# Gated attention, then routed experts: V as the stationary operand of the sums, squares moving 512 wide, and x turned back on its way through DRAM

## The chip, the cores and the metric

The kernel runs on one core of a Trainium2 chip. The metric is the device time of one execution in microseconds. Three runs of the kernel before took 2653.68 to 2654.44 us, with a median of 2654.0 us.

## The reference

Two stages follow each other. In the first, each of 8 batches has 2496 positions with rows u and v of 256 numbers and z of 64.

```python
scores = (1/S) * z @ z.T              # S = 2496, per batch
attn   = maximum(scores, 0) ** 2      # symmetric, as scores is
x      = u * (attn @ v)               # 8 x 2496 rows of 256
```

In the second, each of the 19968 rows of x goes to one of 8 experts, chosen by a hash of its token.

```python
e      = token_ids * 2654435761 % 8
out[i] = maximum(x[i] @ w1[e], 0) @ w2[e]   # w1: 256 x 1024, w2: 1024 x 256
```

Everything is fp32.

## The kernel before

**Tiles.** The positions of a batch are cut into tiles of P = 128: 19 whole tiles and one of R = 64 (tile TM = 19). Four tiles make a group, so a batch has NG = 5 groups of queries, the last of them with 3 whole tiles and the short one (448 queries). The loop runs over 40 groups (b, g). The word "step" below is one call of `between()`, the point at which the side work is given out; a group has 20 steps, and the variable `i` counts them.

**Scores** (L206 to L223). For a group, TensorE computes z z^T for key tiles that are not known yet: `fresh` (L184) lists the group's own tiles and all later ones. Each bank of 128 keys x 512 queries is cut at zero by ScalarE (L221, some by VectorE, L219) into a tile `a` in SBUF, and squared there in place by ScalarE (`square`, L226 to L241). In the last group the squares of the short query tile go into a tile of their own, `short`.

**The mirror.** The matrix is symmetric. Squares with keys of group a and queries of group g are also needed with the roles changed, so VectorE turns each tile of 512 x 512 in blocks of 32 x 32 into a tile `m` (L244 to L256, 16 transposes of 32 partitions x 512). Blocks within a group are turned in place (`own_turns`, L258 to L279). The turns wait in the list `to_turn`. `turn_scores` (L283) takes them off at each step by a budget in nanoseconds, 1450 a step while the sort runs and 1600 after it, at (elements + 170) each; `turn_now` (L294) does at once those that a sum is about to need.

**The sums** (`attend`, L333). For each key tile t and each query tile i, the square tile (128 keys x 128 queries) is the stationary operand, and V's 256 columns are the moving one:

```python
nc.tensor.matmul(acc[i // 2][:, i % 2, :], lhs(b, g, t, i), v_sb[b][:, t, :], ...)
```

The result has queries in the partitions. Two banks `acc` hold the four query tiles of a group. The first two key tiles (EARLY) and the last three (LATE) are done bank by bank, so that one bank can be emptied while the other is still in use. The short key tile is added by `attend_last` (L324), its two copies in the lower and upper 64 rows of the array. The short query tile is summed apart, in `attend_short` (L305), with 64 columns of the array for even and 64 for odd key tiles, and put together in `gate_short` (L314).

**The gate** (L341). VectorE multiplies a query tile of `acc` by u and by 1/S^2 into `x_sb`. GpSimd later scatters its rows with an indirect DMA to the row of `x_rows` in DRAM that the token's place in its expert gives (`place_x`, L557).

**The sort** (`places`, L380 to L541) computes these places in small operations, a few in each of the first 52 steps (SORT), on VectorE and GpSimd, with six small matmuls (L429).

**Loads.** SyncE issues them in the order of the program: z and V of the next batch at the groups 2 and 0, u of the next group at each group's start, the clearing of `x_rows` in the first 52 steps, and from the last group on the experts' weights (`load_w`, L621) and rows (`load_x`, L612).

**The experts** (from L703). Blocks of 512 rows, each followed by a block of 128 rows, each with one expert. `ups` (L725) computes h in banks of 512 columns with w1 as the stationary operand (L735), emptied by ScalarE (even) and VectorE (odd, L741); `down` (L744) multiplies by w2 (L747), ScalarE copies the result, and GpSimd scatters it to the output (L759). `turn_x` (L633) turns a block of x into the layout that `ups` needs. The first block may be read before the last group's rows are in place; in that case it is computed once more at the end.

Of the kernel before, what the change touches and what calls it, by code (L numbers as in the profile page):

```python
# [24 lines left out]
def kernel(  # L25
# [42 lines left out]
    c2 = (1.0 / S) ** 2  # L68
# [13 lines left out]
    xpool = pool("xpool", 3)  # L82

# [3 lines left out]


    slot_dram = nc.dram_tensor("slot_tokens", (P * NS,), I32)


    short = const.tile([P, T, R], F32)
    odd = const.tile([R, D], F32)
# [4 lines left out]
    nc.gpsimd.memset(short[R:P, TM, :], 0.0)  # L98
# [24 lines left out]
    zn, zT, v_sb, u_sb, x_sb, made, mirror, to_square, to_turn, gated = {}, {}, {}, {}, {}, {}, {}, [], [], []  # L123
# [24 lines left out]
    def load_v(b):  # L148
        v_sb[b] = vpool.tile([P, T, D], F32, name="v_sb")
        for g in range(NG):  # L150
            tiles_io(vf, b, group(g), v_sb[b][:, g * G:, :], False, nc.sync, twice=True)
# [21 lines left out]

    def whole(g):

        return range(G if g < NG - 1 else G - 1)
# [5 lines left out]


# [9 lines left out]
    def skipped(b, g, t):  # L193

        if t // G != g or b == 0 and not fine(g):
            return 0
        return (t % G if fine(g) else t % G // 2 * 2) * P

    def fine(g):


        return g > 1
# [3 lines left out]
    def scores(b, g):  # L206

        n = sum(width(t) for t in group(g))
# [17 lines left out]
    def square(n):  # L226
        for b, g, t in to_square[:n]:
            a = made[b, g, t // G][:, t % G, :]
            m = len(whole(g)) * P
            lo = skipped(b, g, t)  # L230
            pairs = [(a[:, lo:m], a[:, lo:m])] if lo < m else []
            if m < G * P:
                pairs.append((short[0:width(t), t, :], a[0:width(t), ds(m, R)]))
            for o, x in pairs:
                nc.scalar.square(o, x)  # L235
            if t % G == G - 1 and (t // G > g or b or fine(g)):
                turns = turns_of(b, g, t // G) if t // G > g else own_turns(b, g)
                to_turn.extend((n, (b, g, t // G), f) for n, f in turns)

                to_turn.sort(key=lambda e: min(e[1][2] - g, 2 if fine(g) else 1))  # L240
        del to_square[:n]  # L241


    def turns_of(b, a, g):  # L244

        def turn(r, c, m):
            if (b, a, g) not in mirror:
                mirror[b, a, g] = mirrors.pop(0)
            nc.vector.transpose(  # L249
                mirror[b, a, g][ts(c, Q)].rearrange("p t s q -> p (t s) q")[:, 0:m, ts(r, Q)],  # L250
                made[b, a, g][ts(r, Q)].rearrange("p t (s q) -> p (t s) q", q=P)[:, 0:m, ts(c, Q)])
        for r in range(NQ):
            for c in range(NQ):

                m = (len(group(g)) if r * Q < width(group(g)[-1]) else G - 1) * G
                yield m * Q, lambda r=r, c=c, m=m: turn(r, c, m)  # L256

    def own_turns(b, g):  # L258
# [7 lines left out]
        for r in range(NQ):  # L266
            for c in range(NQ):
                i, o = ts(r, Q), ts(c, Q)
                if g < NG - 1:
                    yield move(tiles[o, 2:4, 0:2, ts(r, Q)].rearrange("p s i q -> p i s q"), tiles[i, 0:2, 2:4, ts(c, Q)], 4)  # L270
                    if fine(g):
                        yield move(step[o, 0:3:2, ds(3 * P + r * Q, Q)], step[i, 0:3:2, ts(c, Q)], 2)
# [3 lines left out]
                if c * Q < R:  # L276

                    yield move(tiles[o, 3, 0:2, ts(r, Q)], short[i, ds(g * G, 2), ts(c, Q)], 2)
                    yield move(tiles[ds(R + c * Q, Q), 3, 2, ts(r, Q)], short[i, g * G + 2, ts(c, Q)], 1)  # L279
# [3 lines left out]
    def turn_scores(steps):  # L283
# [4 lines left out]
        while to_turn and turned > 0:  # L288
            n, _, f = to_turn.pop(0)
            f()  # L290
            turned -= n + 170
        turned = min(turned, 0)

    def turn_now(key):  # L294
        for e in [e for e in to_turn if e[1] == key]:
            to_turn.remove(e)
            e[2]()

    def lhs(b, g, t, i):

        if t in fresh(b, g):
            return made[b, g, t // G][:, t % G, ts(i, P)]
        return mirror[b, t // G, g][:, i, t % G, :]

    def attend_short(b):  # L305

        ps = mm_ps.tile([P, D], F32, name="q_ps", tag="mm")
        for t in range(T):
            a = short[:, t, :] if t in fresh(b, NG - 1) else lhs(b, NG - 1, t, G - 1)[:, 0:R]
            nc.tensor.matmul(ps[ds(t % 2 * R, R), :], a, v_sb[b][:, t, :],  # L310
                             start=(t < 2), stop=(t >= T - 2), skip_group_check=True)
        return ps

    def gate_short(b, ps):  # L314
        nc.scalar.copy(odd[:], ps[R:P, :])
        x = x_sb[b, NG - 1] = xpool.tile([P, G, D], F32, name="x_sb")
        nc.vector.tensor_add(odd[:], odd[:], ps[0:R, :])
        nc.vector.scalar_tensor_tensor(out=x[0:R, G - 1, :], in0=odd[:], scalar=c2, in1=u_sb[b, NG - 1][0:R, G - 1, :],
                                       op0=OP.mult, op1=OP.mult)
        gated.append((b * T + TM, x[0:R, G - 1, :]))  # L320

    def attend_last(b, g, acc):  # L324

        turn_now((b, TM // G, g))
        for i in (0, 2, 1, 3):
            if i in whole(g):
                h = ds(i // 2 * R, R)
                nc.tensor.matmul(acc[i // 2][:, i % 2, :], lhs(b, g, TM, i)[h], v_sb[b][h, TM, :],  # L330
                                 start=False, stop=False, skip_group_check=True)

    def attend(b, g, k, acc, queries):  # L333
        t = summed(b, g)[k]
        turn_now((b, t // G, g))
        for i in queries:
            if i in whole(g):
                nc.tensor.matmul(acc[i // 2][:, i % 2, :], lhs(b, g, t, i), v_sb[b][:, t, :],  # L338
                                 start=(k == 0 and i % 2 == 0), stop=(k == TM - 1), skip_group_check=True)

    def gate(b, g, i, acc):  # L341
        if i not in whole(g):
            return
        if (b, g) not in x_sb:
            x_sb[b, g] = xpool.tile([P, G, D], F32, name="x_sb")
        x = x_sb[b, g]
        nc.vector.scalar_tensor_tensor(  # L347
            out=x[:, i, :], in0=acc[i // 2][:, i % 2, :], scalar=c2, in1=u_sb[b, g][:, i, :],
            op0=OP.mult, op1=OP.mult,
        )  # L350
        gated.append((b * T + g * G + i, x[:, i, :]))
# [28 lines left out]
    def places():  # L380

        with tc.tile_pool(name="route", bufs=1) as route:
# [20 lines left out]
            room = sorting[:].rearrange("p t s q -> p (t s q)")  # L403
# [15 lines left out]
            yield  # L419
# [3 lines left out]
            yield  # L423
# [144 lines left out]
    nc.scalar.copy(odd[0:1, 0:1], zero[0:1, 0:1])  # L568
# [4 lines left out]
    load_v(0)  # L573
    load_tokens()
    load_u(0, 0)
# [7 lines left out]
    groups = [(b, g) for b in range(B) for g in range(NG)]  # L583
    place = places()
# [3 lines left out]
    def between():  # L588

        nonlocal i  # L590
        if i < SORT:
# [28 lines left out]
    def load_w(j, k):  # L620
        w1[j] = w_buf[2 * k][:].rearrange("p a b c -> p (a b c)").rearrange("p (h f) -> p h f", h=DP)  # L621
        w2[j] = w_buf[2 * k + 1][:].rearrange("p a b c -> p (a b c)").rearrange("p (c d) -> p c d", c=FP)
# [15 lines left out]
    mirrors = [mpool.tile([P, G, G, P], F32, name=f"m_{k}") for k in range(NG * NG // 4)]  # L638
# [3 lines left out]
    for n, (b, g) in enumerate(groups):  # L642
        if n + 1 < len(groups):
            load_u(*groups[n + 1])
        if g == 0 and b + 1 < B:
            load_v(b + 1)
        if g == 2 and b + 1 < B:
# [4 lines left out]
        acc = [acc_ps.tile([P, 2, D], F32, name="acc", tag="acc") for _ in range(2)]  # L652
# [185 lines left out]
```

## Time and profile before

| what | value |
|---|---|
| median of 3 runs | 2654.0 us |
| the profiled execution | 2655.1 us |
| its span, first to last instruction | 2653.2 us |
| granted TensorE clock, mean | 0.999 |
| first matmul of the sums | 17.9 us |
| first matmul of the experts | 1533.5 us |
| VectorE busy, 392 to 1488 us | 881 of 1096 us |
| ScalarE busy, same stretch | 324 of 1096 us |
| GpSimd busy, same stretch | 234 of 1096 us |

The profile is of one execution. A row of a group gives line, engine, operation, output and inputs by name, shape, count, then busy time and mean duration of one, and the idle time before. A row in order of time gives start, length and how many instructions it merges. TensorE shows two records for each fp32 matmul, and its weight loads stand as PEld. [...] A row of a stretch gives busy time and, in brackets, instructions of PE, PEld, DVE, ACT and POOL, then the granted clock, the share of the DMA engines' time and GB/s.

### The profile page before, as it was taken

What the parts mean: (1) busy time and instruction counts of PE and PEld (TensorE: products, weight loads), DVE (VectorE), ACT (ScalarE), POOL (GpSimd) and SP (SyncE); (2) the same over time, 40 slices, a digit from 0 to 9 for tenths busy, and PEclk for the clock granted to TensorE, in tenths of its full rate; (3) what the DMA queues carried; (4) which work ended last, traced back from release to release, by engine and by line L of the source; (5) the groups of instructions that cost most, each with busy time, mean ns of one, the idle gap of its engine ahead of it and who ended that gap; (6) DMA issues with size and microseconds to landing.
All of it is one profiled execution on the core that took longest, in us unless ns stands there. A gap on an engine that the chain in (4) does not pass through costs nothing. (4 is left out here: it accounts for less than half of the span.)

```text
span 2653.2 us, 32524 instructions
## 1 busy us (share of the span) xinstructions
PE 2643.0 (100%) x12054; PEld 2072.2 (78%) x12054; DVE 1394.5 (53%) x2907; ACT 598.1 (23%) x1304; POOL 495.9 (19%) x512
## 2 busy tenths in 40 slices
PE   9999999999999999999999999999999999999999
PEld 7788888888888888888878867777777777777777
DVE  7987888878878877887869811111111111111111
ACT  5115214222233133133142111111111111111111
POOL 1322122212221222222200111111111111111112
PEclk9999999999999999999999999999999999999999
DMA  4212112201220221112101276666666666666662
GB/s 167 63 32 71 39 30 70 51 21 67 51 71 17 51 71 39 37 63 52 33 18 31 63 184 165 162 156 161 154 155 157 155 152 165 164 165 163 166 156 84
DMA packets 288992, 256.74 MB, mean 97 GB/s; under 512 B 179100, under 2 KB 251821, under 8 KB 288832
## 3 DMA queue, kind: packets, MB, share of 16 engines
q1 hardware_dynamic: 268096, 213.55, 32.1%
q0 software_dynamic: 20736, 41.09, 4.6%
q8 instruction: 96, 1.57, 0.3%
q14 instruction: 64, 0.52, 0.1%
HBM read 208.91 MB, written 47.09 MB: 96 GB/s over the span
## 5 line engine op out<-in xcount | busy, mean ns | idle before, releaser
L249 DVE STREAM_TRANSPOSE m<-a 32x512 f32<-32x512 f32 (+1 forms) x1280 | 865.1, 676 | 21.0 <-ACT a L235 0.9
L338 PE MATMUL acc<-v_sb,a 128*128 128x256 f32 x3472 | 764.9, 380 | 0.0
L338 PEld LDWEIGHTS acc<-v_sb,a 128*128 128x128 f32 x3472 | 656.2, 190 | 96.9 <-issue 6.7
L741 DVE TENSOR_SCALAR hT<-h_ps 128x512 f32<-128x512 f32 x161 | 111.4, 692 | 946.2 <-PE h_ps L735 924.1
L735 PE MATMUL h_ps<-v_sb,m 128*128 128x128 f32 (+1 forms) x2080 | 567.7, 431 | 1.5 <-PEq L799 1.5
L747 PE MATMUL o_ps<-m,hT 128*128 128x256 f32 x2576 | 566.3, 379 | 0.0
L747 PEld LDWEIGHTS o_ps<-m,hT 128*128 128x128 f32 x2576 | 486.9, 190 | 77.6 <-issue 14.4
L338 PE MATMUL acc<-v_sb,m 128*128 128x256 f32 x2304 | 504.6, 380 | 2.8 <-DVE x_sb L347 2.8
L735 PEld LDWEIGHTS h_ps<-v_sb,m 128*128 128x128 f32 x2080 | 317.6, 191 | 235.6 <-issue 230.6
L338 PEld LDWEIGHTS acc<-v_sb,m 128*128 128x128 f32 x2304 | 438.7, 190 | 63.6 <-DVE x_sb L347 3.6
L221 ACT ACTIVATE a<-s_ps 128x512 f32<-128x512 f32 (+3 forms) x456 | 205.4, 592 | 851.1 <-PE s_ps L213 851.0
L557 POOL DMA_INDIRECT x_rows<-x_sb,slot_i x160 | 156.2, 976 | 1064.1 <-DVE x_sb L347 886.4
L759 POOL DMA_INDIRECT out_dram<-o_sb,idx x157 | 153.4, 977 | 918.1 <-ACT o_sb L754 910.1
L235 ACT ACTIVATE a<-a 128x512 f32<-128x512 f32 (+3 forms) x472 | 232.8, 651 | 0.0
L265 DVE STREAM_TRANSPOSE a<-a 32x128 f32<-32x128 f32 (+1 forms) x992 | 221.6, 248 | 8.8
L213 PE MATMUL s_ps<-zT 64*128 64x512 f32 (+1 forms) x960 | 195.0, 545 | 0.3 <-ACT zT L171 0.3
L754 ACT COPY o_sb<-o_ps 128x256 f32<-128x256 f32 x161 | 59.9, 372 | 595.4 <-PE o_ps L747 595.4
L739 ACT ACTIVATE hT<-h_ps 128x512 f32<-128x512 f32 x161 | 96.1, 597 | 368.8 <-PE h_ps L735 362.0
L213 PEld LDWEIGHTS s_ps<-zT 64*128 64x128 f32 x960 | 120.3, 186 | 71.2 <-issue 41.5
L545 POOL DMA_INDIRECT slot_tokens<-token,addr x160 | 156.1, 976 | 74.8 <-issue 48.5
L347 DVE SCALAR_TENSOR_TENSOR x_sb<-acc,u_sb 128x256 f32<-128x256 f32 x152 | 57.8, 420 | 194.3 <-PE acc L338 194.1
L635 DVE STREAM_TRANSPOSE v_sb<-v_sb 128x1024 f32<-128x1024 f32 (+1 forms) x65 | 53.9, 829 | 3.6 <-DMA v_sb<-x_rows 3.5
(101 smaller groups left out, 293.4 us busy)
## 6 DMA issues: line engine op xcount, KB each, us to landing
m<-in_moe_w_dram SPq DMA_DIRECT2D x260, 256.0 KB
m<-in_moe_w_dram SPq DMA_DIRECT2D x65, 1024.0 KB
v_sb<-in_v_dram SPq DMA_DIRECT2D x32, 512.0 KB
u_sb<-in_u_dram SPq DMA_DIRECT2D x32, 512.0 KB
v_sb<-x_rows SPq DMA_DIRECT2D x128, 128.0 KB
zn<-in_z_dram SPq DMA_DIRECT2D x28, 304.0 KB
v_sb<-x_rows SPq DMA_DIRECT2D x132, 32.0 KB
x_rows<-zero SPq DMA_DIRECT2D x8, 512.0 KB
```

What stands on the lines that cost most here:

```text
L213: nc.tensor.matmul(ps[:, lo:n], zT[b][h, ts(t, P)], zT[b][h, ds(g * G * P + lo, n - lo)], start=True, stop=True)
L221: nc.scalar.activation(a, ps[:, lo:n], AF.Relu)
L235: nc.scalar.square(o, x)
L249: nc.vector.transpose(mirror[b, a, g][ts(c, Q)].rearrange("p t s q -> p (t s) q")[:, 0:m, ts(r, Q)], made[b, a, g][ts(r, Q)].rearrange("p ...
L265: return n * Q, lambda: nc.vector.transpose(out, in_)
L338: nc.tensor.matmul(acc[i // 2][:, i % 2, :], lhs(b, g, t, i), v_sb[b][:, t, :], start=(k == 0 and i % 2 == 0), stop=(k == TM - 1), skip_gr ...
L545: st = nc.gpsimd.indirect_dma_start(out=slot_dram[:, None], out_offset=bass.IndirectOffsetOnAxis(ap=addr[0:n, c:c + 1], axis=0), in_=token ...
L557: st = nc.gpsimd.indirect_dma_start(out=x_dram[:, :], out_offset=bass.IndirectOffsetOnAxis(ap=slot_i[0:width(c % T), c:c + 1], axis=0), in ...
L735: nc.tensor.matmul(ps[:, ts(i, n)], w1[j][:, c, ts(k * m + i, P)], xT[j][:, :, c, :], start=(c == 0), stop=(c == DP - 1))
L741: nc.vector.tensor_scalar_max(o, ps[:], 0.0)
L747: nc.tensor.matmul(ps[:], hT[j][f][:, ts(t, P)], w2[j][:, f, :], start=(f == 0), stop=(f == FP - 1))
L759: st = nc.gpsimd.indirect_dma_start(out=out[:], out_offset=bass.IndirectOffsetOnAxis(ap=rows, axis=0), in_=o, in_offset=None, bounds_check ...
```

## The change

The roles in the sums change. V is now the stationary operand, and the squares move. V has 256 columns and the array 128, so the even columns go to one bank and the odd ones to the other, and all 512 queries of a group move at once. The result has V's columns in the partitions and queries along the bank: x comes out turned.

- `attend` and `attend_last` issue two matmuls for a key tile in place of four. In the last group of a batch a bank takes 448 queries in two matmuls of 256 and 192, and the short query tile is no longer summed apart: `attend_short`, `gate_short`, `short` and `odd` are gone.
- The queries in a bank are ordered by blocks of 32 rows (`p r i q`), and the mirror tiles have the layout `[P, NQ, G, G, Q]`, so that a turn writes 512 elements in one run. The turns are taken column first.
- The factor 1/S is put into the square.
- The gate turns each bank in blocks of 32 x 32 with VectorE into `x_q`, whose two halves are interleaved. Four DMAs write `x_q` to one of two DRAM buffers `x_way`, and three steps later four DMAs read it back as rows into `x_sb`, and GpSimd multiplies by u, one tile at a time. For the last group half of these DMAs are issued by ScalarE and VectorE multiplies.
- V of the next batch is loaded in five pieces in the groups 1 to 4 (V_LOADS), z in group 3, u at key tile 8 of its own group.
- The sort's pause before its counts is six steps in place of two.
- The weights of the second block of experts are loaded after the loop. The second block of experts starts when all of the first block's downs have been issued.
- `turn_scores` skips a turn for which no mirror tile is free. `CARRIED` is empty, so the path through `carry` is not used.

```diff
     def square(n):
         for b, g, t in to_square[:n]:
-            a = made[b, g, t // G][:, t % G, :]
-            ...
-            for o, x in pairs:
-                nc.scalar.square(o, x)
+            a = made[b, g, t // G][:, t % G, skipped(b, g, t):queries(g)]
+            nc.scalar.activation(a, a, AF.Square, scale=1.0 / S)
...
+    def squares(b, g, t):
+        if t in fresh(b, g):
+            a = made[b, g, t // G][:, t % G, :].rearrange("p (i r q) -> p r i q", r=NQ, q=Q)
+        else:
+            a = mirror[b, t // G, g][:, :, :, t % G, :]
+        parts, c = [], 0
+        for r in ([slice(0, NQ)] if TM not in group(g) else [slice(0, R // Q), slice(R // Q, NQ)]):
+            m = G if r.start < R // Q else G - 1
+            n = (r.stop - r.start) * m * Q
+            parts.append((slice(c, c + n), a[:, r, 0:m]))
+            c += n
+        return parts
...
-        for i in queries:
-            if i in whole(g):
-                nc.tensor.matmul(acc[i // 2][:, i % 2, :], lhs(b, g, t, i), v_sb[b][:, t, :],
-                                 start=(k == 0 and i % 2 == 0), stop=(k == TM - 1), skip_group_check=True)
+        for h in halves:
+            for cols, a in squares(b, g, t):
+                nc.tensor.matmul(acc[h][:, cols], v_sb[b][:, t, h::2], a,
+                                 start=(k == 0 and cols.start == 0), stop=(k == TM - 1), skip_group_check=True)
...
+    def gate(b, g, h, acc):
+        n = queries(g) // Q
+        if h == 0:
+            x_q[b, g] = qpool.tile([P, G * NQ, D // NQ], F32, name="x_q")
+        x = x_q[b, g]
+        nc.vector.transpose(x[:, 0:n, h::2], acc[h][:, 0:n * Q].rearrange("p (n q) -> p n q", q=Q))
+        if h == 0:
+            return
+        xs = xpool.tile([P, G, D], F32, name="x_sb")
+        o = x_way[g % len(x_way)]
+        ends = (b, g) == groups[-1]
+        queues = [nc.sync, nc.scalar if ends else nc.sync]
+        for a in range(NQ):
+            queues[a % 2].dma_start(o[:].rearrange("n p d -> p n d")[:, 0:n, ts(a, D // NQ)], x[ts(a, Q), 0:n])
+        def rows_of_x():
+            c = 0
+            for r in range(NQ):
+                m = G if r * Q < width(group(g)[-1]) else G - 1
+                queues[r % 2].dma_start(xs[ts(r, Q), 0:m], o[c:c + m].rearrange("i p d -> p i d"))
+                c += m
+            for k, t in enumerate(group(g)):
+                y = xs[0:width(t), k, :]
+                (nc.vector if ends else nc.gpsimd).tensor_mul(y, y, u_sb[b, g][0:width(t), k, :])
+                gated.append((b * T + t, y))
+        to_fetch.append((i + 3, None, rows_of_x))
...
-            yield
-            yield
+            for _ in range(6):
+                yield
...
+    V_LOADS = [(4, 4), (1, 9), (2, 9), (3, 6), (3, 12)]
...
             for t in range(TM - LATE, TM):
-                attend(b, g, t, acc, [2 * k, 2 * k + 1])
-            for q in (2 * k, 2 * k + 1):
-                gate(b, g, q, acc)
+                attend(b, g, t, acc, [k])
+            gate(b, g, k, acc)
...
+            if first < i == AHEAD:
+                while do:
+                    do.pop(0)()
...
+    load_w(work[1], 1)
     load_x(work[1], 1)
     run(work, 0, NM, NM + 2)
```

## The prediction

> **What bounds the kernel now.** I read the engine totals first, then who waits for whom, then the order of time on TensorE at a few places, then stretches. The totals, from part 1 of the page:
>
> ```profile
> PE 2643.0 (100%) x12054; PEld 2072.2 (78%) x12054; DVE 1394.5 (53%) x2907; ACT 598.1 (23%) x1304; POOL 495.9 (19%) x512
> ```
>
> TensorE is busy for 2643.0 of 2653.2 us. The list of waits holds only three entries with PE as the waiter worth a microsecond: 2.8 us for the gate's VectorE, 1.5 us at a branch, 1.2 us at the start. So a change can gain in two ways only: fewer or cheaper TensorE passes, or those few waits. Work on the other engines counts only where it newly makes TensorE wait. Each fp32 matmul appears as two records (two passes), so 19 key tiles x 4 query tiles are 152 records.
>
> What a pass costs is not its mean duration (380 ns is a latency; passes overlap) but the step from one start to the next. Rows of TensorE in order of time (start, length, count), from two stretches:
>
> ```profile
> 1550.76 13.98 PE L747 MATMUL o_ps<-m,hT 128*128 128x256 f32 x64
> ...
> 1533.46 8.75 PE L735 MATMUL h_ps<-v_sb,m 128*128 128x512 f32 x20
> ```
>
> 256 wide: (13.98 - 0.38 for the last one)/63 = 215.9 ns. 512 wide: (8.75 - 0.59)/19 = 429.5 ns. A pass of double width costs double: 431.8 against 429.5, 2.3 ns apart. Weight loads last 190 ns and hide under either. This decides the size of the case: moving squares 512 wide halves the instructions and loads of weights, but removes only those 2.3 ns for each pair of passes.
>
> **The sums, full groups.** 8 batches x 4 groups x 76 passes of 512 replace twice as many of 256: 2432 x 2.3 = 5.6 us less. The group rows would say otherwise:
>
> ```profile
> L338 PE MATMUL acc<-v_sb,a 128*128 128x256 f32 x3472 | 764.9, 380 | 0.0
> ...
> L735 PE MATMUL h_ps<-v_sb,m 128*128 128x512 f32 x1024 | 449.6, 592 | 1.5 <-PEq L799 1.5
> ```
>
> 449.6/1024 = 439.1 against 2 x 220.3 = 440.6, a gain of 3.6 us; with the mirror row (504.6/2304 = 219.0) it is a loss of 2.7 us. These rows count the tail of every run of passes in two groups at once, so I take the steps in time, and keep 0 as the other end.
> The moving squares are read in runs of 32 elements, as L735's xT already is at 429.5 ns, so I cost that at nothing.
>
> **The last group of a batch (448 queries).** Before: 114 passes x 215.9 = 24.6 us, and the 40 half-width passes of attend_short. In time, 24 of these took 2.69 us (1525.72 to 1528.41), so 40 take 4.5 us; together 29.1. After: 76 pairs of a 256- and a 192-wide pass. No row is 192 wide. The small block's 32 passes of 128 follow 32 of 512 in one run of 17.47 us: (17.47 - 0.28 - 32 x 0.4295)/31 = 111 ns. Halfway between 111 and 215.9 is 164 ns, and 76 x 379.9 = 28.9 us. Gain 0.2 us a batch, 1.8 us in all (0 to 3 by the roundness of these).
> The last key tile (L330) took 0.96 us a group (621.26 to 622.22). After, four passes of 512 run two at a time, as the scores do: 32 passes in 6.74 us (622.22 to 628.96), so 4 are 0.84, plus about 0.1 for entering the half-row form, which both have. I take 0, with -3.8 us as the other end.
>
> **Weights with a stride of 8 bytes.** V's even or odd columns are read every second element; no row of before has this. If it costs nothing, loads can follow each other every 111 ns (the 128-wide run shows it), below every pass. [...] If [...] the load took twice 111 = 222 ns, the full groups would still hide it (429.5), but the last group would not: max(215.9, 222) + max(164, 222) = 444 instead of 380, 64 ns x 608 pairs = 39 us. I take 0, because [...] the load has 190 ns of latency to spare under most passes.
>
> **VectorE.** Removed: 152 gates of 424 ns and 16 short ones (57.8 + 6.6 = 64 us). Added: 80 turns of a PSUM bank, 512 wide. Nearest rows: a transpose 128x512 takes 703 ns, an operation that reads 512 from PSUM 692 ns; 80 x 0.7 = 56 us. The turns of scores keep number and size (0.70 us); only their order and output layout move. VectorE is 80% busy in the steady stretch, so the total doesn't matter, but the moment does. The group boundary near 255 us:
>
> ```profile
> 255.02 3.19 PE L338 MATMUL acc<-v_sb,m 128*128 128x256 f32 x14
> 255.22 0.76 DVE L347 SCALAR_TENSOR_TENSOR x_sb<-acc,u_sb 128x256 f32<-128x256 f32 x2 [1.10 <-PE acc L338]
> ```
>
> The second bank is emptied by 255.98. TensorE starts the next group on the first bank at 255.02 and needs the second eight passes (1.73 us) later, at 256.75: slack 0.77 us. One turn of 0.70 to 0.76 us in place of two gates fits the same hole; a turn up to about 1.5 us would.
>
> ScalarE loses the short square and copy and gains nothing on the path; with 598 us busy I cost it at 0. GpSimd gains 160 multiplies. Its 1280-wide ones took 2.3 to 2.9 us, so 0.6 us each, 100 us hidden under 2150 us of idle time. They wait for DMAs, and sort operations and scatters queue behind them; nothing on TensorE needs those before the experts. SyncE gains 8 DMAs a group. The writes wait for VectorE's turn and the reads for the writes, and loads of u, v, z stand behind them; V is now loaded in five pieces 10 or more steps (17 us) ahead of its use, and u eleven steps. Cost 0.
>
> **The one stall, at 98 us.** Two stretches there:
>
> ```profile
> 98.00:104.00 6.00, 3.17 (x14) 2.15 (x13) 5.91 (x9) 2.84 (x7) 0.00 (x0) 1.00 0.00 0
> 104.00:110.00 6.00, 6.00 (x21) 4.94 (x21) 5.78 (x15) 0.00 (x0) 0.61 (x1) 0.72 0.67 145
> ```
>
> TensorE idled 2.83 us because VectorE was behind with turns and the sort, and the clock then fell to 0.72 for 6 us (1.7 us). Altogether 4.5 us. In the change the sort starts its counting four steps later. In VectorE's order the same 41 turns lie between the gates of the first two groups, with seven small operations more (7 x 0.2 = 1.4 us), while the 2.31 us reduction (L529) moves behind the second gate. First wait 0.5 + 1.4 = 1.9, second 2.5 - 2.3 + about 0.2 = 0.4: 2.3 instead of 2.8, the clock's share unknown. I take -1.0; ends -4.5 and +2.
>
> **Into the experts.** Now the last group's x goes out, comes back, is multiplied and only then scattered; the second block's weights are loaded after the loop. Before, the chain from the last gate (1533.66) to the second block's x in place was 7.7 us:
>
> ```profile
> 1541.32 0.45 DVE L635 STREAM_TRANSPOSE v_sb<-v_sb 128x256 f32<-128x256 f32 x1 [3.53 <-DMA v_sb<-x_rows]
> ```
>
> After: turn 0.7, write and read, each like that x load (issue 1538.07 to 1541.32, 3.3 us), four multiplies of 0.42, then the same 7.7: about 17 us. TensorE has 13.7 us of block 0's up and 13.8 us of its down first (27.5 us), and the downs are all put ahead of block 1. But VectorE waits inside this chain until about 9.5 us, with the emptying of h_ps behind it: with six banks of 1.72 us TensorE needs bank 1 back at 12.0 us. Slack 2.5 us. [...] The x rows go out in pieces of 256 bytes. The nearest row, the 256-byte loads above, is a read. By that row the slack stays 2.5 us[...]. 2 MB of weights at the 160 GB/s of that stage is 13 us, done by about 20. I take +0.5 (0 to +4).
>
> **Sum.** -5.6 - 1.8 - 1.0 + 0.5 = -7.9 us. The profiled execution took 2655.1 us (span 2653.2 and 1.9 around), so it becomes 2647.2; it lies 1.1 above the median, so the forecast is 2646 us.
>
> **Rivals.**
> A (forecast, 0.57): 2646, from 2642 to 2648.
> B (0.13): the stall at 98 us goes with its clock drop and the last key tile gains a little: -7.4 - 4.5 = about 2641. For it: the reduction has left the place between the gates. Against: more small work ahead of the first.
> C (0.14): the gain is real but spent elsewhere; entry to the experts +3, stall +1.5: about 2651. For it: chain slack of only 2.5 us. A change that does nothing measurable is this case too.
> D (0.11), other side: strided weights load at half rate. Place: the last group's 192-wide passes; price 39 us; 2646 + 39 = 2685. It turns the sign once the pair takes 393 ns, that is when loads step by about 177 ns, 1.6 times the 111. [...]
> E (0.05): the PSUM turn with its strided output takes 2 us, not 0.7: beyond 1.5 each boundary stalls, 0.5 x 39 = 20 us: 2666. Against: both nearest rows at 0.7.
>
> Faster by over 0.2% means below 2648.7: A and B, 0.70. C gives 0.14 within 0.2%, about what a measurement of this kernel can tell from no change. D and E give 0.16 slower. The range runs from 2637 (B with both unknown ends) to 2656 (C with its bounds) and leaves out D and E.
>
> **What would show it.** Right: 512-wide passes of the sums step by 429 to 430 ns, last-group pairs by about 380; no wait of TensorE for the turn beyond the one near 98 us; clock near 1.0. Wrong: pairs over 393 ns (D); a wait for the turn at every boundary (E); a gap of TensorE within 30 us of the experts' start (C); steps in the full groups that aren't 2 ns below two old ones, in which case the whole gain is missing.

## The result, and the profile after

The change made the kernel a little faster: 2645.2 us (median of 8 runs, 2643.37 to 2646.51) against 2653.9 (8 runs, 2653.44 to 2654.44). The ratio is 0.9967, with a 95% interval of 0.9956 to 0.9978. The profiled execution took 2645.0 us, its span is 2643.3 us, and the mean granted clock is 0.999, as before. The forecast was 2646 us.

The totals of the page after:

```profile
PE 2633.5 (100%) x9494; PEld 1627.3 (62%) x9494; DVE 1398.2 (53%) x2823; ACT 593.4 (22%) x1272; POOL 605.9 (23%) x667
```

TensorE executes 2560 records fewer, a fifth of the 12054, and is busy only 9.5 us less. VectorE is where it was, GpSimd gained 110 us. TensorE's rows of the sums, by form (count, then busy time and mean length of one):

```profile
L353 PE MATMUL acc<-a,v_sb 128*128 128x512 f32 x1664 | 728.7, 594 | 0.0
...
L353 PE MATMUL acc<-m,v_sb 128*128 128x256 f32 x512 | 152.3, 379 | 0.0
...
L353 PE MATMUL acc<-m,v_sb 128*128 128x192 f32 x512 | 125.1, 326 | 0.0
```

The lengths of one (594, 379, 326 ns) overlap and don't add up to the time; the steps do. TensorE in order of time (start, length, count), two runs of passes around the first group boundary and one in a last group:

```profile
101.41 15.59 PE L353 MATMUL acc<-m,v_sb 128*128 128x512 f32 x32 [2.89 <-DVE x_q L370]
116.84 13.90 PE L353 MATMUL acc<-a,v_sb 128*128 128x512 f32 x32
...
174.59 24.38 PE L353 MATMUL acc<-m,v_sb 128*128 128x256 f32 x128
```

The second row gives the new step: (13.90 - 0.59)/31 = 429.4 ns, against 431.8 for two old passes. The third row merges passes 256 and 192 wide in equal numbers: (24.38 - 0.38)/127 = 189 ns on average, or 378 for a pair. The first row is the one stall, and in the list of who waits for whom it is the only entry of more than 1.2 us with PE waiting:

```profile
PE acc L353 <- DVE x_q L370: 2.9, 1, 2.9
PE warm L611 <- POOL zero L96: 1.2, 1, 1.2
PE h_ps L775 <- ACTq L844: 0.9, 1, 0.9
```

By stage, read from the starts of the instructions (us). A batch runs from its first score matmul to that of the next one:

| stage | before | after | difference |
|---|---|---|---|
| start to the first score matmul | 8.76 | 8.68 | -0.08 |
| first batch, with the stall | 192.89 | 191.09 | -1.80 |
| six batches, each | 189.62 | 188.50 | -1.12 (-6.7 for six) |
| last batch, to the first expert matmul | 194.12 | 193.25 | -0.87 |
| experts | 1119.76 | 1119.27 | -0.49 |
| span | 2653.2 | 2643.3 | -9.9 |

Within a steady batch the four full groups give 4 x 0.18 = 0.73 us (the steps of a group's sums add up to 32.82 instead of 33.00), the sums of the last group 0.31, and the rest, with the last key tile, 0.09. The gain is there, small and evenly spread. The medians differ by 8.7 and the spans by 9.9, because the profiled execution before lay 1.2 us above its median.

The group boundary, VectorE in order of time (idle time and what ended it in brackets):

```profile
289.23 0.72 DVE L370 STREAM_TRANSPOSE x_q<-acc 128x512 f32<-128x512 f32 x1 [4.53 <-PE acc L353]
289.98 1.42 DVE L253 STREAM_TRANSPOSE m<-a 32x512 f32<-32x512 f32 x2
...
291.80 0.72 DVE L370 STREAM_TRANSPOSE x_q<-acc 128x512 f32<-128x512 f32 x1 [0.40 <-PE acc L353]
```

VectorE waits for TensorE before it turns each of the two banks, so here it isn't late; in all, it waits so before 71 of the 80 banks. Two turns of scores lie between the two banks, a detail that comes back below.

### The profile page after: what moved, and what is told of

It is laid out like the page before. It is cut to its first block, busy times and chain, and to the rows that moved or that the text cites. A ratio compares the mean times of both kernels' runs of the same rounds, so it can differ in the third digit from the quotient of the medians.

```text
span 2643.3 us, 27985 instructions
## 1 busy us (share of the span) xinstructions
PE 2633.5 (100%) x9494; PEld 1627.3 (62%) x9494; DVE 1398.2 (53%) x2823; ACT 593.4 (22%) x1272; POOL 605.9 (23%) x667
## 4 chain that ended last, share of the span: by engine, by line
PE 56%; issue 35%; POOL 6%; DVE 2%; POOLq 0%; DMA 0%; ACT 0%; ACTq 0%; SPq 0%; DVEq 0%
PE acc L353 47%; PE s_ps L219 7%; POOL out_dram L799 6%; PE acc L362 2%; DVE m L253 1%; POOLq L799 0%; PE warm L611 0%; DMA x_way<-x_q 0%; DMA x_sb<-x_way 0%; POOL x_rows L597 0%; DVE x_q L370 0%; DVE per_e L533 0%; DVE zn L525 0%; DVE per_e L537 0%; POOL v_sb L757 0%
## 5 line engine op out<-in xcount | busy, mean ns | idle before, releaser
L353 PE MATMUL acc<-a,v_sb 128*128 128x512 f32 (+2 forms) x1856 | 766.1, 570 | 0.0
L353 PEld LDWEIGHTS acc<-a,v_sb 128*128 128x128 f32 x1856 | 357.5, 196 | 378.8 <-issue 364.6
L353 PE MATMUL acc<-m,v_sb 128*128 128x512 f32 (+2 forms) x1792 | 530.2, 456 | 2.9 <-DVE x_q L370 2.9
L353 PEld LDWEIGHTS acc<-m,v_sb 128*128 128x128 f32 x1792 | 335.6, 197 | 196.7 <-issue 180.8
L389 POOL TENSOR_TENSOR x_sb<-x_sb,u_sb 128x256 f32<-128x256 f32 (+1 forms) x156 | 108.4, 724 | 928.1 <-DMA x_sb<-x_way 928.1
L280 DVE STREAM_TRANSPOSE a<-a 32x128 f32<-32x128 f32 (+2 forms) x1120 | 250.2, 248 | 10.2
L235 ACT ACTIVATE a<-a 128x512 f32<-128x512 f32 (+1 forms) x480 | 233.0, 646 | 0.0
L219 PEld LDWEIGHTS s_ps<-zT 64*128 64x128 f32 x960 | 110.2, 186 | 93.0 <-issue 62.9
L370 DVE STREAM_TRANSPOSE x_q<-acc 128x512 f32<-128x512 f32 (+1 forms) x80 | 56.3, 704 | 188.7 <-PE acc L353 188.4
```

The costliest lines, as they stand in the source:

```text
L219: nc.tensor.matmul(ps[:, lo:n], zT[b][h, ts(t, P)], zT[b][h, ds(g * G * P + lo, n - lo)], start=True, stop=True)
L235: nc.scalar.activation(a, a, AF.Square, scale=1.0 / S)
L280: return n * Q, lambda: nc.vector.transpose(out, in_)
L353: nc.tensor.matmul(acc[h][:, cols], v_sb[b][:, t, h::2], a, start=(k == 0 and cols.start == 0), stop=(k == TM - 1), skip_group_check=True)
```

## The experiments

Each experiment changes the kernel after; its ratio compares its median with that of the kernel before on the same chip. Chips differ a little: the kernel before took 2654.2 to 2655.6 us on those used here.

**Squares 256 wide again.** The change with its 512 columns moved in two parts:

```diff
-        for r in ([slice(0, NQ)] if TM not in group(g) else [slice(0, R // Q), slice(R // Q, NQ)]):
-            m = G if r.start < R // Q else G - 1
+        for r in [slice(0, R // Q), slice(R // Q, NQ)]:
+            m = G if r.start < R // Q or TM not in group(g) else G - 1
```

> The changed kernel, its squares moving 256 wide: V still stands, every key tile of a full group takes two matmuls for each half of V. Theory (a pass costs its columns and a fixed 2.5 ns, so width gives the full groups their gain): 2432 passes of 429.2 ns become 4864 of 215.9, so 2.5 ns each, +6.1 us; the last group is unchanged. Span 2649 us, clearly nearer to the kernel before. Rival (the gain comes from V standing still, from the boundaries or from the other engines, and width is nothing): no difference, span 2643 us.

Measured: 2651.2 us, ratio 0.9988 (0.9981 to 0.9994), 6.0 above the change (5.7 when each is set against the kernel before on its own chip); a steady batch takes 189.28 us, 0.78 more. In order of time:

```profile
307.64 13.98 PE L353 MATMUL acc<-a,v_sb 128*128 128x256 f32 x64
```

64 passes fill 13.98 us where 32 wide ones fill 13.90: (13.98 - 0.38)/63 = 215.9 ns. So the width of the moving operand is worth the 2.3 ns a pair, and this makes up most of the result.

**Columns of V without a stride.** Each bank takes 128 columns side by side in place of every second one, in both sums; the columns of x are then in another order.

```diff
-                nc.tensor.matmul(acc[h][:, cols], v_sb[b][:, t, h::2], a,
+                nc.tensor.matmul(acc[h][:, cols], v_sb[b][:, t, ts(h, P)], a,
```

> The changed kernel, but the halves of V are columns 0 to 127 and 128 to 255, read without a stride; the columns of x come out in another order. Theory (a stride of 8 bytes is free): time within 1 us of the changed kernel, 192-wide passes at 160 to 164 ns as now; weight loads may fall from 196 to 190 ns, which is hidden. Rival (the stride costs something, in the 192-wide passes of the last group): 608 pairs get faster by some ns each, a gain of 1 to 3 us.

**Every fourth column.** The weights have a stride of 16 bytes and reach into the next key tile, so the sums are of other numbers (the last key tile stays as it is).

```diff
-                nc.tensor.matmul(acc[h][:, cols], v_sb[b][:, t, h::2], a,
+                nc.tensor.matmul(acc[h][:, cols], v_sb[b][:].rearrange("p t d -> p (t d)")[:, t * D + h:t * D + h + 4 * P - 3:4], a,
```

> The changed kernel, but each weight load of the sums takes every fourth element of V (16 bytes apart, over two key tiles), so the sums are of other numbers; attend_last keeps its stride of 8 bytes. Theory A ([...] at least double): loads step by 222 ns or more, full groups hide it, last-group pairs go from 378 to at least 444 ns, +40 us or more, span 2683 us or above. Theory B ([...] the stride is nothing): span 2643 us, last-group pairs at 378 ns.

Measured: 2644.2 us without a stride (0.9962, 0.9948 to 0.9976), and 2703.7 us with 16 bytes (1.0186, 1.0170 to 1.0201). The rows of weight loads, of the change, of no stride, and of 16 bytes (last but one number: mean ns of one):

```profile
L353 PEld LDWEIGHTS acc<-a,v_sb 128*128 128x128 f32 x1856 | 357.5, 196 | 378.8 <-issue 364.6
```

```profile
L353 PEld LDWEIGHTS acc<-a,v_sb 128*128 128x128 f32 x1856 | 346.6, 190 | 389.1 <-issue 372.6 <-ACT a L235 7.4 <-ACT a L227 3.8
```

```profile
L353 PEld LDWEIGHTS acc<-a,v_sb 128*128 128x128 f32 x1856 | 555.1, 311 | 199.3 <-issue 6.4
```

Eight bytes cost 6 ns a load and next to no time: a batch takes 188.50 against 188.42 us, 0.7 us for all eight. Sixteen cost 121 ns a load. Where it hurts is seen in a last group with 16 bytes, TensorE in order of time:

```profile
179.66 26.01 PE L353 MATMUL acc<-m,v_sb 128*128 128x256 f32 x111
```

(26.01 - 0.37)/110 = 233 ns a pass where the change has 189: here the load, not the pass, sets the step. The theory's doubling, to 222 ns or more, was my own estimate, twice the 111 ns at which 128-wide passes stepped before, and comes near. In the full groups it is hidden: passes still step by (19.91 - 0.59)/45 = 429 ns, read at 619.68 us. A batch is 7.2 us longer, 58 for eight. So the slower load that the prediction feared shows at 16 bytes, where it sets a step of 233 ns, and not at 8, where the last group steps by 189. Why 16 bytes are slow and 8 are not, no run shows.

**No way through DRAM.** The eight DMAs of a group are left out, and GpSimd multiplies what the gate wrote by u as it lies, so the products aren't rows of x.

```diff
-        for a in range(NQ):
-            queues[a % 2].dma_start(o[:].rearrange("n p d -> p n d")[:, 0:n, ts(a, D // NQ)], x[ts(a, Q), 0:n])
...
-                queues[r % 2].dma_start(xs[ts(r, Q), 0:m], o[c:c + m].rearrange("i p d -> p i d"))
...
-                (nc.vector if ends else nc.gpsimd).tensor_mul(y, y, u_sb[b, g][0:width(t), k, :])
+                k0 = k if t < TM else 0
+                z = x[0:width(t), k0 * NQ:k0 * NQ + NQ].rearrange("p n d -> p (n d)")
+                (nc.vector if ends else nc.gpsimd).tensor_mul(y, z, u_sb[b, g][0:width(t), k, :])
```

> The changed kernel without the way through DRAM: GpSimd multiplies the turned tile x_q itself by u, so the rows that are scattered are not the rows of x. All eight DMAs a group are gone. Theory (the detour is wholly hidden): span within 1 us of 2643.3; at the experts' start VectorE is free about 9 us earlier, with nothing gained. Rival (the detour's DMAs slow weights, squares or the experts' entry): a gain of 2 us or more.

Measured: 2645.2 us, ratio 0.9967 (0.9954 to 0.9979), the change's own time, with batches of 188.50 us. The detour is wholly hidden.

**The detour's DMAs twice.** Each write and each read is issued a second time.

```diff
-        for a in range(NQ):
+        for a in [*range(NQ)] * 2:
...
-                queues[r % 2].dma_start(xs[ts(r, Q), 0:m], o[c:c + m].rearrange("i p d -> p i d"))
+                for _ in range(2):
+                    queues[r % 2].dma_start(xs[ts(r, Q), 0:m], o[c:c + m].rearrange("i p d -> p i d"))
```

> The changed kernel, each of the detour's DMAs issued twice. Theory: nothing in the groups; at the experts' start the chain of write and read gets about 3 us longer, VectorE comes back to h_ps at about 14 us in place of 10.9 after the first expert matmul, TensorE needs bank 1 at 12.0 us and waits 2 to 3 us once; span about 2646 us. Rival (DMA traffic itself is in the way of TensorE or of loads): losses spread over the groups, 5 us or more, and waits of TensorE for DMAs. Second rival (slack larger than reckoned): 0.

Measured: 2664.0 us, ratio 1.0036 (1.0023 to 1.0050). The six batches between still take 188.50 us; the loss is the last batch, 202.74 instead of 193.25, the experts, 1128.7 instead of 1119.3, and 1.6 us in the first batch. But the main place isn't the one expected. TensorE's longest wait and, below it, SyncE's issues in order of time:

```profile
PE h_ps L776 <- DVE v_sb L679: 9.3, 1, 9.3
```

```profile
1504.10 11.00 SPq L386 DMA_DIRECT2D x_sb<-x_way  x8
...
1528.69 1.92 SPq L660 DMA_DIRECT2D v_sb<-x_rows  x4
```

TensorE waits 9.3 us at its first expert matmul, for block 0's x (v_sb), not at bank 1. The eight reads hold SyncE for 11.00 us, because each second read waits until the first has landed in the same tile (SyncE's list of waits has `x_sb<-x_way` 8 times there, 15.8 us in all). Their rows are scattered later, and the load of block 0, which waits for that scatter in both kernels (8.5 us here, 9.3 without the doubling), is issued at 1528.7 us instead of 1515.6. That chain had been on no list of mine. In the experts TensorE then waits 1.8 us for a bank and 2.5 us for weights, and its first 24 passes take 13.1 us. So a bank is waited for, as expected, but one of ScalarE's, and for less time than block 0's x.

**The same, but not in the last two groups.**

```diff
-        for a in [*range(NQ)] * 2:
+        for a in [*range(NQ)] * (2 if groups.index((b, g)) < len(groups) - 2 else 1):
...
-                for _ in range(2):
+                for _ in range(2 if groups.index((b, g)) < len(groups) - 2 else 1):
```

> The detour's DMAs doubled in all groups but the last two. Theory (the loss of the doubled run came at the experts' entry alone, by the last two groups: x of the group before last is scattered later, so block 0's x comes too late): span within 2 us of 2643.3, no wait of TensorE at the first expert matmul. Rival (the doubled traffic costs in the groups): about 2655 us or more.

Measured: 2681.6 us, ratio 1.0092 (1.0077 to 1.0108), on a chip on which the kernel before took 2655.6. The end behaves as the theory said: the last batch takes 193.26 us, and no wait stands before the first expert matmul. But the steady batches took 191.1 to 196.6 us, 34 us more in all, with waits of the sums for squares and for the turns of banks:

```profile
PE acc L353 <- ACT a L235: 12.2, 6, 2.8
PE acc L353 <- DVE x_q L370: 6.9, 8, 4.2
```

The run before had the same doubling in the same groups and 188.50 us in each batch, so the doubled traffic as such, the rival here, isn't shown to be the cause. What differs in the traces is ScalarE: while it cuts scores at zero between 220 and 1500 us it stands still 37 times, for 0.2 to 1.5 us, 24.6 us in all, where the run before has not one such stop. Near 405 us, for one, its scores were ready, and SyncE's issues and VectorE's turns of z stood as in the run before, which speaks against late loads. What it waited for the profile doesn't name. From this pair only the place of the first one's loss is taken.

**Each bank turned twice, and three times.** The edit for twice; three times has `range(3)`.

```diff
-        nc.vector.transpose(x[:, 0:n, h::2], acc[h][:, 0:n * Q].rearrange("p (n q) -> p n q", q=Q))
+        for _ in range(2):
+            nc.vector.transpose(x[:, 0:n, h::2], acc[h][:, 0:n * Q].rearrange("p (n q) -> p n q", q=Q))
```

> The changed kernel, each bank turned twice into the same tile, so that emptying a bank takes 1.43 us of VectorE in place of 0.72. Theory (the second bank has 0.8 us of slack at each group boundary): no stall at the boundaries, only the one near 98 us longer by about 1 us; span 2643 to 2645 us. Rival (VectorE is already at its limit at 80%, and any work added to it shows): 80 x 0.72 = 57 us more work, a loss of 10 us or more.

> The changed kernel, each bank turned three times, 2.15 us. Theory: the second bank is then late by 2.15 - 0.72 - 0.8 = 0.65 us at each of 39 boundaries, some 25 us in all, span about 2669 us, and the list of waits names TensorE waiting for the turn at every boundary. Rival (the slack is larger[...]): under 5 us.

Measured: twice 2664.2 us (1.0038, 1.0024 to 1.0051), three times 2720.0 us (1.0247, 1.0231 to 1.0263). Both are dearer than the theory's slack allowed. TensorE's waits, first with each bank turned twice, then three times (us in total, times, longest):

```profile
PE acc L353 <- DVE x_q L371: 11.5, 25, 4.3
```

```profile
PE acc L353 <- DVE x_q L371: 60.9, 40, 4.7
```

And one boundary with each bank turned twice, VectorE and TensorE in order of time:

```profile
293.06 1.47 DVE L371 STREAM_TRANSPOSE x_q<-acc 128x512 f32<-128x512 f32 x2 [3.97 <-PE acc L353]
294.56 1.42 DVE L253 STREAM_TRANSPOSE m<-a 32x512 f32<-32x512 f32 x2
...
296.01 1.47 DVE L371 STREAM_TRANSPOSE x_q<-acc 128x512 f32<-128x512 f32 x2
...
297.63 1.53 PE L353 MATMUL acc<-m,v_sb 128*128 128x512 f32 x3 [0.32 <-DVE x_q L371]
```

From the start of the first bank's turn to TensorE's need of the second bank are 297.63 - 0.32 - 293.06 = 4.25 us (six passes for the late key tiles and four for the early ones, about 10 x 0.43). In it must fit two gates, the two turns of scores between them, and small gaps: 2T + 1.42 + 0.21. That gives a limit of T = 1.31 us, not 1.5, because the first bank's turn and the scores delay the second's. At T = 1.47 the sum is over by the 0.32 us of this wait, from which it was read. The test is three times (2.15 to 2.2): over by some 1.7 us a boundary by this sum, and a steady batch grew by 9.15 us, 1.8 for each of its five boundaries.

**Twice, with the turns of scores moved behind the second bank.** Beside the doubling:

```diff
-            turn_scores(1 if k else 0.8)
+            if k:
+                turn_scores(1.8)
```

> Each bank turned twice as before (1.43 us), but the turns of scores that stood between the two banks' turns are handed out after the second. Theory (in the doubled run the second bank was late because first bank's turn 1.43 + two score turns 1.43 = 2.86 us did not fit in the 2.58 us in which TensorE does the last three key tiles of the second half; without them the second turn starts on time and ends 1.63 us after the next group's first pass, 0.1 us before it is needed): the waits at the boundaries vanish, only the first stall near 98 us is longer than in the changed kernel, by 1 to 2 us; span 2644 to 2647 us. Rival (VectorE's total load decides): still about 2660 us.

Measured: 2663.0 us, ratio 1.0030 (1.0019 to 1.0041). The waits at the boundaries are nearly gone, 4 in place of 25:

```profile
PE acc L353 <- DVE x_q L371: 6.8, 4, 4.8
```

Yet the time is only 1 us better (2 us by the ratios), and over 14 us above the theory. The first batch took 196.0 us where doubling alone took 194.2. Five of the six steady batches took 189.7 to 190.0 us, where doubling alone took 190.6 and the change 188.5, and one took 191.2, on the chip that also made the batches of the early doubling uneven. So the two turns between the banks seem to account for 0.8 of the 2.1 us that doubling costs a steady batch. At three boundaries of one of these batches the second bank is still late: its first two passes step by 0.53 and 0.51 us in place of 0.43. That moving the turns pays isn't shown.

**The stall: turns held back, and given back.** In the group with the stall, VectorE's budget for turns is cut at three steps; in the second kernel it is given back over six later ones.

```diff
-        turned += steps * (1600 if i >= SORT else 1450)
+        turned += steps * (0 if 33 <= i < 36 else 1600 if i >= SORT else 1450)
```

```diff
-        turned += steps * (1600 if i >= SORT else 1450)
+        turned += steps * ({33: 700, 34: 0, 35: 0}.get(i, 1600 if i >= SORT else 1450)) + (682 if i in (44, 47, 50, 60, 64, 68) else 0)
```

> The changed kernel with no turns handed out in the three steps before the end of the second group (steps 33 to 35), about six turns of 0.71 us moved behind that gate. Theory (the stall near 98 us is VectorE's queue of turns and sort work ahead of the gate; 4.4 us late at the first bank): the wait and the clock's dip go, -4 to -4.7 us, span about 2639 us, unless the turns held back make the next boundary late (then up to 2 us of it are lost). Rival (the stall is the sort's own chain, or would be paid later in full): span 2643 us or more.

> The changed kernel with about five turns held back in the three steps before the end of the second group, and six handed out again one by one in the third and fourth group (steps 44 to 68), where VectorE was seen idle for 2.9 and 2.8 us. Theory (the stall near 98 us is only the order of VectorE's work, and the earlier attempt lost its gain because the six turns stayed behind to the end of the batch): no stall near 98 us and none near 194 us; span about 2638.6 us, 4.5 us below the changed kernel. Rival (VectorE has no room in the first batch, and the debt comes up wherever it is put): a wait of 2 to 4 us at another boundary, span 2642 us or more.

Measured: 2646.5 us (0.9969, 0.9956 to 0.9981) and 2647.0 us (0.9964, 0.9951 to 0.9978). TensorE's wait after each, in the first and in the second:

```profile
PE acc L362 <- DVE a L280: 3.6, 1, 3.6
```

```profile
PE acc L353 <- DVE x_q L370: 2.0, 1, 2.0
```

The stall near 98 us is gone in both. In the first, a wait of 3.6 us stands at 194 us in its place, with VectorE busy for 5.76 of the 6 us from 192 us on: the turns held back were never given back, and the batch's last turns came late. In the second, a wait of 2.0 us stands at 172 us. It looks like the same debt, and its time is the rival's, but the stretch shows another thing (busy time of PE, PEld, DVE, ACT, POOL):

```profile
170.00:174.00 4.00, 2.40 (x11) 1.56 (x9) 1.61 (x4) 0.00 (x0) 1.50 (x2) 1.00 0.01 0
```

VectorE is busy for 1.61 of 4 us. It stood idle for 2.34 us before the turn that TensorE waited for, and the profile doesn't name what it waited for, as with ScalarE's stops in the early doubling, on the same chip. So the first kernel speaks for turns put off and not given back being paid later; that VectorE has no room in the first batch isn't shown by either.

**Where VectorE's time went.** VectorE, then GpSimd, of the kernel after in order of time, some 14 us before the stall:

```profile
83.92 1.60 DVE L533 TENSOR_TENSOR per_e<-m,per_e 128x8 f32<-128x8 f32 x1
85.56 0.17 DVE L534 TENSOR_TENSOR per_e<-per_e 128x8 f32<-128x8 f32 x1
...
86.99 1.52 DVE L537 TENSOR_TENSOR per_e<-per_e 128x8 f32<-128x8 f32 x1
```

```profile
83.18 2.32 POOL L536 TENSOR_TENSOR zn<-zn,per_e 128x1280 f32<-128x1280 f32 x1
85.58 2.90 POOL L540 TENSOR_TENSOR zn<-zn 128x1280 f32<-128x1280 f32 x1
```

Operations of one size, 128x8, take 0.17 us or nine times that. The long ones end with GpSimd's: 83.92 + 1.60 = 85.52 against 83.18 + 2.32 = 85.50, and 88.51 against 88.48. Two transposes on VectorE, with one input each, take 1.30 us meanwhile, as two took at 86.22 us in the kernel before, where GpSimd ran nothing. The kernel before has the same: its L493 took 1.93 us and its L497 1.31 us, beside the same two GpSimd operations. That the long ones waited for GpSimd's to end is read from the ends that fall together; why they would, no trace shows. So 1.43 + 1.35 = 2.8 us of VectorE's time are lost just ahead of a stall of 2.9.

**The sort's small operations out of the way.** One comparison goes ahead of GpSimd's long operations; the three others on the same tile go to GpSimd itself; the small operations that follow from their result go to the end of the sort.

```diff
+            nc.vector.tensor_tensor(late, upto[:, :, C - G - 1], thr, op=OP.is_ge)
             nc.vector.tensor_tensor(total, rank, wide(thr), op=OP.is_ge)
...
-            nc.vector.tensor_tensor(late, ahead, thr, op=OP.is_ge)
-            nc.vector.tensor_mul(late, late, jump)
+            nc.gpsimd.tensor_mul(late, late, jump)
...
-            nc.vector.tensor_add(late, late, start)
-            nc.vector.tensor_add(late, late, ahead)
+            nc.gpsimd.tensor_add(late, late, start)
+            nc.gpsimd.tensor_add(late, late, ahead)
```

> The changed kernel with the sort's small operations of two inputs taken out of GpSimd's way: the comparison (L533) stands ahead of GpSimd's long operations, the product and two sums that follow are done by GpSimd itself, and the minimum, the flags and the count come at the end of the sort. What is computed is the same. In the changed kernel L533 and L537 took 1.60 and 1.52 us in place of 0.17 and ended with a GpSimd operation each; VectorE is 4.4 us late at the second group's gate. Theory ([...] this makes the stall near 98 us): about 4.2 us leave VectorE's queue ahead of that gate, nothing is owed later, the stall and the clock's dip go; span 2638 to 2639.5 us, 13 to 15 us below the kernel before on the same chip. Rival (VectorE has no room in the first batch whatever is moved): the wait shrinks but appears again at a later gate, span 2641 us or more.

Measured: 2641.2 us (2641.14 to 2642.43), ratio 0.9950 (0.9937 to 0.9964), 4.0 below the change (5.0 when each is set against the kernel before on its own chip) and the best of all. The profiled span, 2639.4 us, is where the theory put it. The stall is gone, not moved. The stretch around it (busy time and instructions of PE, PEld, DVE, ACT, POOL, then clock), first of the change, then of this kernel:

```profile
97.00:103.00 6.00, 3.11 (x6) 1.23 (x5) 5.77 (x10) 3.44 (x8) 0.00 (x0) 0.85 0.00 0
103.00:109.00 6.00, 6.00 (x13) 2.64 (x12) 5.87 (x8) 0.00 (x0) 0.00 (x0) 0.86 0.48 87
```

```profile
97.00:103.00 6.00, 6.00 (x15) 2.75 (x14) 5.86 (x9) 2.93 (x7) 0.00 (x0) 1.00 0.48 87
```

TensorE runs through, the clock stays at 1.00, and the first batch takes 186.35 us, 4.7 less. Some 1.0 us of it is lost again in the later batches (188.5 to 188.9 us instead of 188.50). The comparison, on VectorE in order of time, takes 0.17 us again, at a moment when GpSimd runs nothing (its next operation starts at 80.31 us):

```profile
78.66 0.17 DVE L525 TENSOR_TENSOR per_e<-m,per_e 128x8 f32<-128x8 f32 x1
```

Between the first two groups' gates VectorE's sort operations took 7.3 us in place of 11.4. Of the 4.1 us less, 2.8 are what the two operations took beyond 0.17 us and 1.3 the operations' own time, which also went elsewhere; the run doesn't part the two.

## Why the prediction was right, step by step

**Full groups, -5.6.** Measured -5.8 (32 x 0.18), confirmed by undoing the width alone (+6.0, or 0.78 a steady batch). The choice to read steps and not the mean length of one was decisive; a fifth of the instructions gone looked like far more.

**Last group, -1.8, and last key tile, 0.** The direction was right, the size small: 8 x 0.31 = -2.5 for the sums, and -0.7 for the rest of the group, which I had put at 0. The 192-wide pass steps by about 162 ns, not 164, and that term, halfway between two rows, was the estimated one.

**Strided weights, 0 (rival D, +39).** Right, to within 0.7 us. A stride of 8 bytes left the mean load at 196 ns, where it is 190 without a stride; one of 16 bytes made it 311. The pair that I feared (444) was about 466 there, two passes of 233.

**The gate's turn.** 718 ns on average, inside the predicted 0.70 to 0.76, so rival E fell. The remark that a turn of up to about 1.5 us would fit was wrong: it took the second bank alone. The first bank's turn and two turns of scores share the hole, and the limit is 1.3.

**The stall, -1.0.** The group with it became 0.45 us shorter beyond the gain of every group, so the step failed in size. TensorE's wait is 2.9 us where it was 2.8, and the clock's dip costs 1.7 us in both kernels: 32 passes took 15.59 us where the next 32 took 13.90. The split into 1.9 and 0.4 us failed too: one wait of 2.9 us for the first bank, none for the second. The reduction did leave, as I had it, and took the second wait along. But with seven operations more, VectorE's sort work between the two gates went from 9.3 to 11.4 us, 2.1 more and not the 1.4 that I gave them at 0.2 us each. The two that ended with a GpSimd operation are not the reason, since they took 3.2 us before and 3.1 after. Rival B's saving was open, for a cause that it didn't name: moving those operations gave 4.0 us.

**The entry to the experts, +0.5.** No gap of TensorE, and the experts started 0.25 us later than a steady batch's gain would have it. But the slack was over-counted. VectorE in order of time:

```profile
1520.48 1.25 DVE L678 STREAM_TRANSPOSE v_sb<-v_sb 128x1024 f32<-128x1024 f32 x1 [5.90 <-DMA v_sb<-x_rows]
...
1533.43 1.49 DVE L389 TENSOR_TENSOR x_sb<-x_sb,u_sb 128x256 f32<-128x256 f32 x4 [8.57 <-DMA x_sb<-x_way]
...
1545.31 0.45 DVE L678 STREAM_TRANSPOSE v_sb<-v_sb 128x256 f32<-128x256 f32 x1 [6.67 <-DMA v_sb<-x_rows]
```

The first expert matmul starts at 1524.0. VectorE is back at 1534.9, 10.9 us after it (9.5 predicted, 12.0 needed): 1.1 us of slack, not 2.5. Block 1's x is turned 21.3 us after it (17 predicted, 27.5 needed). And the first row is a chain that I missed: block 0's x waits for the scatter of the group before the last, is ready at 1521.7, and is needed 2.3 us later. Doubling the DMAs broke that first. The 0.5 us less in the experts is the wait at a branch, 0.9 us now and 1.5 before; it was no part of my sum.

**The detour's price.** I costed the write in pieces of 256 bytes by a read, at 3.3 us, and its time to landing stayed below that. DMA issues (KB each, median us from issue to landing):

```profile
x_sb<-x_way SPq DMA_DIRECT2D x143, 128.0 KB, 2.7
x_way<-x_q SPq DMA_DIRECT2D x128, 128.0 KB, 2.9
```

The writes in pieces of 256 bytes land after 2.9 us, the reads in rows of 1 KB after 2.7. No run here shows what the pieces cost in bandwidth, and leaving the detour out gained nothing. GpSimd's multiply took 724 ns, not 0.6 us, hidden as predicted:

```profile
L389 POOL TENSOR_TENSOR x_sb<-x_sb,u_sb 128x256 f32<-128x256 f32 (+1 forms) x156 | 108.4, 724 | 928.1 <-DMA x_sb<-x_way 928.1
```

**The sum.** -7.9 predicted and -9.9 in spans: more than predicted came from the last groups (-1.4) and, unforeseen, from the branch (-0.5), less from the stall (+0.3 to 0.5); the rest is the entry and rounding. That 2646 lies 0.8 us from the median is in part luck: the sum was 2.0 us short in the spans, with misses of both signs in it.

## What to carry to other kernels

Where TensorE is busy all the time, cost a change by the step from one start to the next: half the passes at twice the width were worth 6 us of 2651. Before a small VectorE operation with two inputs is costed at its own duration, see whether GpSimd runs at that moment; its place may matter more than its size (0.17 us became 1.60 here). A slack is the room for the whole chain between two waits of the bound engine, all the items queued on the way included.

## What the runs showed of the hardware that was not expected

- Two VectorE operations of 128x8 with two inputs each ended within 0.03 us of a GpSimd operation and took 1.60 and 1.52 us in place of 0.17; without GpSimd beside it, the first took 0.17.
- Weights with a stride of 16 bytes made the load step about 233 ns, where 128-wide passes stepped by 111 without a stride; 8 bytes cost 6 ns a load and at most 0.08 us of a batch of 188.5.
- A stall of 2.0 to 2.9 us was followed by half the clock for some 3.4 us. In the kernel after, stretches of 1 us from 101 us on read 0.62, 0.50, 0.50, 0.68 and 1.00, and passes of 512 step by 0.85 us in place of 0.43, which costs 1.7 us beside the wait. The 0.72 over 6 us in the kernel before (after 2.5 us of waiting), the 0.85 and 0.86 here, and 0.72 over 174 to 180 us with the turns given back (after 2.0 us) are means over the same kind of dip.
- On one chip two kernels had uneven batches (191.1 to 196.6 and 189.7 to 191.2 us) where their like had even ones elsewhere. In the first of them ScalarE stood still 37 times, and in a third kernel on that chip VectorE stood still for 2.34 us at 172 us, with no cause that the profile names. The cause stays open.
